# Signs of the second layer's weights put back by VectorE as bits, three small steps free to run on ScalarE or VectorE, and the order drawn anew

## The chip, the cores and the metric

The kernel runs on one core of a Trainium2 chip. A time is the device time of that core in microseconds (us). TensorE (PE) multiplies, VectorE (DVE), ScalarE (ACT) and GpSimd (POOL) do the elementwise work, and SyncE (SP) issues the DMA transfers. TensorE's clock has two levels, 2.4 and 1.2 GHz; the profile gives the granted clock as a share of the upper one.

## The reference, cut to what matters

```python
def reference(q, k, v, w_in, w_out, g_ln, w2_in, w2_out):   # q, k, v: 8 x 8 heads x 576 x 64
    k_p, v_p = mean over groups of 8 positions of k, v       # 72 of them
    attn = softmax(q @ k_p.T / sqrt(64)) @ v_p
    x = attn laid out as 4608 tokens x 512
    h = x @ w_in                                             # 512 x 1024
    solu = h * softmax(h)
    x = (solu - mean) / sqrt(var + 1e-6) * g_ln @ w_out      # 1024 x 512
    h = x @ w2_in                                            # 512 x 2048
    return (h * sigmoid(1.702 * h)) @ w2_out                 # 2048 x 512
```

The inputs arrive as 64-bit floats. A weight is read as pairs of 32-bit words (high word, low word), and a float32 value is made from them in the kernel.

## The kernel before, in words

Each float32 operand of a product is split into two half-precision parts (a high and a low half), and a product is three matmuls (high by high, high by low, low by high).

**The first phase** holds the attention, the first layer and the preparation of the second layer's weights. It runs over 36 tiles of 128 tokens. For a tile t: the scores (TensorE into PSUM tile `psx`), their maximum and the exponential `e`, the sum `rs` of a row of it, `rs` scaled and inverted, `e` times that, its split into the tile `st`, a transposing DMA into `aT`, the product with the values (into PSUM tile `psv`, of which there is one buffer), and its split into the halves of `xT`. Then the first layer's product (into `psh`), its softmax and statistics (`hmx`, `he`, `tt`, `mean`), and for each pair of tiles the normed `zs`, a transposing DMA into `zT`, the product with `w1o` (into `psy`, one buffer) and a copy `y` of it that goes to DRAM.

Weights are prepared beside that. Of a piece `raw` of 128 x 1024 pairs of words ScalarE makes the signs (`sgw`), turns the low words into integers and scales the high words; VectorE shifts and joins them (`scalar_tensor_tensor raw<-raw`), which drops the sign; GpSimd multiplies by `sgw`. For the second layer there are 16 such pieces (`values_of`); the result `w_f` is then combined on GpSimd into seven sums, split into `hi` and `lo`, and written to DRAM as `w2i_dram` and `w2o_dram`. For the first layer (`joined`) there are six more. The scale of a weight needs the largest value of all partitions: a diagonal tile `diag` of the partitions' values is multiplied by ones into `psy` or `psv` (a **spread product**), from where VectorE takes the maximum (`w1o_all`, `galln`, `w2all`, `v_all`).

**The order** of the first phase is drawn by a planner (`Plan`). Every chain of steps is a strand with a due time. `Plan.run` looks at each strand's next operation, estimates from a table of costs when its engine could begin it, adds a part of the slack and a random amount (`DRAWS`: until which planned time of TensorE, how much, which seed), and takes the lowest score. An operation that may run on two engines goes where planned end plus `spare` is earlier. The result is one fixed instruction stream for each engine: an engine runs its stream in order, and an instruction whose input is not there holds up all behind it.

**The second phase** (`Up`, `Down`, from line 1349) is the second layer, written out by hand in blocks of 768 tokens. The change doesn't touch it.

Of the kernel before, what the change touches and what calls it, by code (L numbers as in the profile page):

```python
# [9 lines left out]
F32 = mybir.dt.float32  # L10
F16 = mybir.dt.float16
BF16 = mybir.dt.bfloat16
I32 = mybir.dt.int32
U32 = mybir.dt.uint32
AF = mybir.ActivationFunctionType
ALU = mybir.AluOpType
# [4 lines left out]
P = 128  # L21
# [9 lines left out]
KM = DM // P  # L31
# [11 lines left out]
WC = 512  # L43
# [21 lines left out]
PULL = 900  # L65
HASTE = 0.01
DUE_W_OUT = 40000
SPARE = 3000
DUE_Q = 0
PULL_EARLY = 2  # L70
EARLY_END = 60000
# [5 lines left out]
ALONE = 4  # L77
UPS = 4
DNS = 7
SG = 4  # L80
LAST = 90000
LATE = 3000
LATE_TURN = 3000
TTS = 4
DRAWS = ((70e3, 600, 13), (200e3, 150, 4), (330e3, 150, 13), (1e9, 150, 1))
V_TOP = 2.0 ** 14

TOP3 = 2.0 ** -29 * (1 - 2.0 ** -23)
A_TOP = 2.0 ** 14
# [2 lines left out]
Y_TOP = 2.0 ** 13  # L92
G_DOWN = 2.0 ** -22
TINY = 2.0 ** -100

# [86 lines left out]
class Plan:  # L184
# [31 lines left out]
    def drop(self, *tiles):  # L216
        for t in tiles:
            del self.ring_of[t.name]
# [12 lines left out]
    def estimate(self, op):  # L231
        best = None
        for engine in op.engines:
            t = max(self.free[engine], self.ready(op, engine))
            if engine == "sp":
                t = max(t, self.free["dma"] - 2000)
            if engine == "dve" and op.port and self.pool_from <= t < self.free["pool"]:
                t = self.free["pool"]
            key = t + op.cost[engine] + self.spare[engine] if len(op.engines) > 1 else t
            if best is None or key < best[0]:  # L240
                best = (key, t, engine)
        return best[1:]
# [54 lines left out]
def moe_kernel(ctx: ExitStack, tc: tile.TileContext, qT, kT, vT, w_in, w_out, g_ln, w2_in, w2_out, eye, outT):  # L297
    nc = tc.nc
# [137 lines left out]
    with ExitStack() as ph:  # L436
# [6 lines left out]
        kv = tc.alloc_tile_pool(name="kv", bufs=2, side="right")  # L443
# [12 lines left out]
        plan = Plan()  # L456
        start, drop = plan.start, plan.drop
# [53 lines left out]
        def V(name, *args, **kw):  # L511
            return op(("dve",), name, args, kw)

        def G(name, *args, **kw):
            return op(("pool",), name, args, kw)
# [4 lines left out]
        def A(**kw):  # L520
            return op(("act",), "activation", (), kw)

        def D(dst, src=None, turn=False, short=1):
            pairs = dst if src is None else [(dst, src)]

            def emit(engine):
                for pair in pairs:
                    (nc.sync.dma_start_transpose if turn else nc.sync.dma_start)(*pair)

            outs, ins = ([p[i] for p in pairs] for i in range(2))  # L530
            n = sum(math.prod(x.shape) * mybir.dt.size(x.dtype) for x in outs)
            return Op(("sp",), emit, outs, ins, {"sp": n / 360 * (1.23 if turn else short)}, turn)
# [82 lines left out]
        def values_of(raw, up, dst, begun=None):  # L615

            hw, lw = raw[:, :, 1], raw[:, :, 0]
            sg = yield New(kv, [P, 2 * WC], F16, "sgw", bufs=SG // 2)
            if begun is not None:
                begun.append(sg)  # L620
            yield A(out=sg, in_=hw.bitcast(F32), func=AF.Sign)
            yield A(out=lw.bitcast(U32), in_=lw.bitcast(U32), func=AF.Copy, scale=TOP3, bias=-0.49999)
            yield lambda: (up.name, up.offset) in upped
            yield A(out=hw.bitcast(F32), in_=hw.bitcast(F32), func=AF.Copy, scale=up)
            yield V(
                "scalar_tensor_tensor", out=lw, in0=hw, scalar=3, in1=lw, op0=ALU.logical_shift_left,
                op1=ALU.bitwise_or,
            )
            d = yield from dst()
            yield G("tensor_tensor", out=d, in0=sg, in1=lw.bitcast(F32), op=ALU.mult)  # L630
            drop(sg)

        def raw_new(q, n):
            return New(kv, [P, q, n, 2], I32, "raw", "raw", RAWS)
# [155 lines left out]
        def pooled(kind, b, src, due):  # L790
            yield lambda: b == 0 or begun[kind][b - 1] == 2
            dst = yield New(kv, [P, NPAIR, SP], F32, kind + "p", bufs=1)
# [9 lines left out]
            ps = yield New(psy, [P, 2, YB], F32, "psy", "psy")  # L802
            sums = ps.rearrange("p a c -> p (a c)")[:, : NPAIR * SP].rearrange("p (a s) -> p a s", s=SP)
            for j in range(2):
# [2 lines left out]
                yield T(rows[:4])  # L807
                yield T(rows[4:])
                drop(raws[j])
            yield A(out=dst, in_=sums, func=AF.Copy)  # L810
            drop(ps)
            return dst

# [43 lines left out]
        def attention(t):  # L857
# [10 lines left out]
            ps = yield New(psx, [P, 2, 512], F32, "psx", "psx")  # L868
# [23 lines left out]
            else:  # L892
                yield V(
                    "tensor_tensor", out=e.rearrange("p (a h) k -> p a h k", a=2), in0=s4,
                    in1=m3.unsqueeze(3).to_broadcast([P, 2, 4, SP]), op=ALU.add,
# [2 lines left out]
                yield A(out=e, in_=e, func=AF.Exp)  # L898
            rs = s1("rs", H)
            yield V("tensor_reduce", out=rs, in_=e, axis=AX.X, op=ALU.add)  # L900
            yield A(out=rs, in_=rs, func=AF.Copy, scale=1.0 / A_TOP, bias=1e-9 / A_TOP)
            yield V("reciprocal", rs, rs)
            yield VG("tensor_tensor", out=e, in0=e, in1=rs.unsqueeze(2).to_broadcast([P, H, SP]), op=ALU.mult)
            yield lambda: t < 2 or turned[t - 2]
# [38 lines left out]
            drop(aT)  # L943
            xT = yield New(sb, [P, 2 * KM, P], F16, "xT", bufs=2)
            turned_x = ps.rearrange("p (k t) -> p k t", t=P)
            yield A(out=xT[:, 0:KM], in_=turned_x, func=AF.Copy, scale=1.0 / A_TOP)
            yield V(
                "scalar_tensor_tensor", out=xT[:, KM:], in0=turned_x, scalar=1.0 / A_TOP, in1=xT[:, 0:KM],
                op0=ALU.mult, op1=ALU.subtract,
# [4 lines left out]
        class Pair:  # L954
# [95 lines left out]
            def project(self, half):  # L1050
# [20 lines left out]
                        ]  # L1071
                    )
                y = yield New(sb, [P, 2, YB], F32, "y", bufs=2)
                yield A(out=y, in_=ps, func=AF.Copy)
                drop(drop_ps)
                i, o = divmod(self.i * YB, YD)
                yield D(y_dram[i][:, 2 * half : 2 * half + 2, o : o + YB], y)
# [210 lines left out]
            yield D(eye_t, eye)  # L1288

        plan.early, plan.until = PULL_EARLY, EARLY_END  # L1290
        plan.pull, plan.haste, plan.spare = PULL, HASTE, {"pool": 0.0, "dve": SPARE}

        def due(t):
            return FIRST_STEP + STEP * t
# [430 lines left out]
```

## Time and profile before

| | us |
|---|---|
| median of 3 runs | 1175.5 (1172.25 to 1175.65) |
| the profiled execution | 1171.01 |
| its span in the profile | 1169.0 |
| TensorE busy | 1125.7 (96% of the span) |
| ScalarE, VectorE, GpSimd busy | 754.7, 724.4, 617.7 |

The times in the rows are microseconds from the start of the span. An instruction's idle time stands in brackets with what released it. The second phase begins at about 505 us.

### The profile page before, as it was taken

To read this page: it belongs to the slowest core of one execution; us is meant where nothing else is said; L and a number is where in the kernel's file an instruction comes from. 1 tells how busy PE (TensorE), PEld (TensorE's weight loads), DVE (VectorE), ACT (ScalarE), POOL (GpSimd) and SP (SyncE) were. 2 spreads that over 40 slices of the span, in tenths; PEclk is the share of its full clock that TensorE was granted. 3 is DMA by queue.
4 is the path that set the end of the run, shared out by engine and by line. 5 is a ranking of instruction groups with operands and counts; after the bars stand their busy time and mean duration, and the time that the engine had idled before them with its cause. 6 is when DMAs were issued, how large, how long until landed. Compare 5 with 4: busy or idle time off the path is not lost.

```text
span 1169.0 us, 19696 instructions
## 1 busy us (share of the span) xinstructions
PE 1125.7 (96%) x7737; PEld 726.1 (62%) x7737; DVE 724.4 (62%) x1105; ACT 754.7 (65%) x997; POOL 617.7 (53%) x643
## 2 busy tenths in 40 slices
PE   4888999999999999999999999999999999999998
PEld 4555676667676667765566656666666665566655
DVE  7988888777677753426753773567266636753650
ACT  6889998989798874737624752674367337625740
POOL 4566999989999985315503530561056016403530
PEclk9989999999999999999999999999999999999999
DMA  9979999999999768355465355536453653463131
GB/s 356 277 191 278 243 280 282 278 275 273 270 244 226 178 172 262 85 195 193 146 200 174 125 176 163 180 127 202 142 174 126 214 178 127 149 202 117 60 121 60
DMA packets 247356, 225.75 MB, mean 193 GB/s; under 512 B 165728, under 2 KB 218080, under 8 KB 246752
## 3 DMA queue, kind: packets, MB, share of 16 engines
q1 hardware_dynamic: 247264, 224.50, 67.0%
q8 instruction: 60, 0.98, 0.3%
q14 instruction: 32, 0.26, 0.1%
HBM read 151.06 MB, written 33.55 MB: 158 GB/s over the span
## 4 chain that ended last, share of the span: by engine, by line
PE 69%; POOL 13%; ACT 6%; DVE 5%; DMA 5%; issue 2%; SPq 1%; POOLq 0%; ACTq 0%; DVEq 0%
PE bank_a L1385 31%; PE bank_d L1385 16%; PE bank_b L1385 8%; PE psy L537 6%; PE psh L537 5%; POOL w_f L496 3%; PE psv L537 2%; POOL lo L496 2%; POOL zs L496 2%; POOL st L496 1%; POOL e L496 1%; PE psx L537 1%; DMA w2i_dram<-lo 1%; POOL q L496 1%; DMA raw<-w_out 1%
## 5 line engine op out<-in xcount | busy, mean ns | idle before, releaser
L1385 PEld LDWEIGHTS <-w2o 128*128 128x128 f16 x2016 | 197.0, 98 | 130.4
L1385 PEld LDWEIGHTS <-w2i 128*128 128x128 f16 x1974 | 193.1, 98 | 129.9 <-issue 2.4
L349 POOL TENSOR_TENSOR w_g<-w_g 128x384 f32<-128x384 f32 x42 | 46.1, 1097 | 399.2 <-ACT w_g L1464 399.2
L1479 DVE SCALAR_TENSOR_TENSOR g<-w_g,gu_b,g 128x1152 f16<-128x1152 f32 (+1 forms) x96 | 175.4, 1828 | 92.0 <-ACT g L1474 91.7
L1385 PE MATMUL bank_a<-ys,w2i 128*128 128x384 f16 x1128 | 205.6, 326 | 0.9 <-ACT c L1404 0.9
L537 PE MATMUL psh<-w1i,xT 128*128 128x512 f16 x864 | 201.8, 384 | 3.5 <-ACT xT L496 3.1
L1385 PE MATMUL bank_a<-g,w2o 128*128 128x384 f16 x1152 | 201.6, 326 | 0.0
L537 PEld LDWEIGHTS <-w1o 128*128 128x128 f16 x1728 | 168.0, 98 | 30.8 <-DMA zT<-zs 2.8
L537 PE MATMUL psy<-zT,w1o 128*128 128x256 f16 x1536 | 176.2, 273 | 3.5 <-DMA zT<-zs 2.3
L1474 ACT ACTIVATE g<-w_g,gu_b 128x1152 f16<-128x1152 f32 (+1 forms) x96 | 134.3, 1411 | 50.3 <-POOL w_g L352 39.3
L1404 ACT ACTIVATE c<-bank_a 128x384 f32<-128x384 f32 x188 | 90.7, 483 | 102.4 <-PE bank_a L1385 101.8
L537 PEld LDWEIGHTS <-xT 128*128 128x128 f16 x864 | 83.4, 99 | 96.3 <-issue 6.0
L1385 PE MATMUL bank_d<-g,w2o 128*128 128x384 f16 x576 | 104.2, 326 | 0.0
L496 POOL TENSOR_TENSOR zs<-tt,zs 128x1024 f16<-128x1024 f32 x36 | 78.4, 2178 | 44.2 <-ACT zs L496 43.8
L1385 PE MATMUL bank_d<-ys,w2i 128*128 128x384 f16 x564 | 101.1, 326 | 0.0
L1464 ACT ACTIVATE w_g<-c,ch_b 128x1536 f32<-128x1536 f32 x47 | 73.8, 1570 | 28.7 <-DVE c L1407 28.7
L352 POOL TENSOR_TENSOR w_g<-w_g 128x384 f32<-128x384 f32 x42 | 83.2, 1982 | 0.0
L1407 DVE SCALAR_TENSOR_TENSOR c<-bank_d,c 128x384 f32<-128x384 f32 x94 | 51.9, 552 | 41.9 <-ACT c L1404 29.6
L496 POOL TENSOR_TENSOR lo<-w_f,hi 128x512 f16<-128x512 f32 (+1 forms) x48 | 65.8, 1389 | 6.6 <-ACT e L496 2.9
L496 DVE TENSOR_REDUCE hmx<-psh 128x1 f32<-128x1024 f32 x36 | 43.8, 1218 | 36.2 <-PE psh L537 36.2
L537 PE MATMUL psx<-kbd,qt 128*128 128x144 f32 (+1 forms) x320 | 47.8, 312 | 15.1 <-ACT kbd L496 9.6
L496 DVE CUSTOM_DVE_ANT_0 tt<-psh,he 128x1024 f32<-128x1024 f32 x36 | 43.8, 1218 | 23.1 <-ACT he L496 22.9
(205 smaller groups left out, 1606.8 us busy)
## 6 DMA issues: line engine op xcount, KB each, us to landing
w2i<-w2i_dram SPq DMA_DIRECT2D x48, 896.0 KB, 4.6
w2o<-w2o_dram SPq DMA_DIRECT2D x84, 512.0 KB, 3.7
half<-kT SPq DMA_DIRECT2D x16, 576.0 KB, 6.4
half<-vT SPq DMA_DIRECT2D x16, 576.0 KB, 6.2
qt<-qT SPq DMA_DIRECT2D x36, 256.0 KB, 4.7
y_dram<-y SPq DMA_DIRECT2D x36, 256.0 KB, 3.5
y<-y_dram SPq DMA_DIRECT2D x48, 192.0 KB, 4.0
raw<-w_in SPq DMA_DIRECT2D x16, 512.0 KB, 7.7
```

Source lines behind the costliest of these rows:

```text
L349: eng.tensor_tensor(out=w[:, 1], in0=q[:, Q12], in1=q[:, Q11], op=ALU.subtract)
L352: eng.tensor_tensor(out=w[:, 3], in0=q[:, Q21], in1=w[:, 2], op=ALU.subtract)
L496: getattr(eng, name)(*args, **kw)
L537: nc.tensor.matmul(*p[:3], start=p[3], stop=p[4], skip_group_check=len(p) > 5)
L1385: nc.tensor.matmul(bank, self.weight(p, kk, w), self.data(p, kk, i), start=(first and kk == 0 and w == 0 and i == 0), stop=(last and kk == ...
L1404: nc.scalar.activation(out=self.c[:, i], in_=getattr(self, bank), func=AF.Copy, scale=self.scale)
L1407: nc.vector.scalar_tensor_tensor(out=self.c[:, i], in0=getattr(self, bank), scalar=self.scale, in1=self.c[:, i], op0=ALU.mult, op1=ALU.add,)
L1464: nc.scalar.activation(out=self.w[:, 0:4], in_=self.c, func=AF.Gelu_apprx_sigmoid, scale=self.ch)
L1474: nc.scalar.activation(out=self.g[s.start][:, 0], in_=self.w[:, s], func=AF.Copy, scale=self.gu)
L1479: nc.vector.scalar_tensor_tensor(out=self.g[s.start][:, 1], in0=self.w[:, s], scalar=self.gu, in1=self.g[s.start][:, 0], op0=ALU.mult, op1 ...
```

## The change

The signs of the 16 second-layer pieces are no longer made by ScalarE and multiplied in by GpSimd. After the join, a second `scalar_tensor_tensor` on VectorE takes the sign bit of the high word and ors it into the joined word, on its way from `raw` to `w_f`. The first layer's six pieces keep their `sgw`, now with four buffers in place of two. Three kinds of operations that were ScalarE's alone may now be put on VectorE by the planner, with a reserve (`SPARE_ACT`) of 500: the copies out of PSUM into `y` and the pooled keys and values, the first half of `xT`, and the scaling of `rs`. The seeds of the draws are new, and there are six stretches of them in place of four.

```diff
+SPARE_ACT = 500
-SG = 4
+SG = 8
-DRAWS = ((70e3, 600, 13), (200e3, 150, 4), (330e3, 150, 13), (1e9, 150, 1))
+DRAWS = (
+    (70e3, 600, 15), (160e3, 150, 15), (320e3, 150, 777820), (360e3, 150, 313302), (450e3, 150, 383972),
+    (1e9, 150, 372027),
+)
+SIGN = -(2 ** 31)
...
-            key = t + op.cost[engine] + self.spare[engine] if len(op.engines) > 1 else t
+            key = t + op.cost[engine] + self.spare[op.engines[0], engine] if len(op.engines) > 1 else t
...
+        def AD(out, in_, scale=None):
+            def emit(engine):
+                if engine == "act":
+                    nc.scalar.activation(out=out, in_=in_, func=AF.Copy, **({} if scale is None else {"scale": scale}))
+                elif scale is None:
+                    nc.vector.tensor_copy(out, in_)
+                else:
+                    nc.vector.tensor_scalar_mul(out, in_, scale)
...
+        def rescaled(rs):
+            def emit(engine):
+                if engine == "act":
+                    nc.scalar.activation(out=rs, in_=rs, func=AF.Copy, scale=1.0 / A_TOP, bias=1e-9 / A_TOP)
+                else:
+                    nc.vector.tensor_scalar(
+                        out=rs, in0=rs, scalar1=1.0 / A_TOP, scalar2=1e-9 / A_TOP, op0=ALU.mult, op1=ALU.add
+                    )
...
         def values_of(raw, up, dst, begun=None):
-            sg = yield New(kv, [P, 2 * WC], F16, "sgw", bufs=SG // 2)
-            yield A(out=sg, in_=hw.bitcast(F32), func=AF.Sign)
...
-            yield G("tensor_tensor", out=d, in0=sg, in1=lw.bitcast(F32), op=ALU.mult)
-            drop(sg)
+            yield V(
+                "scalar_tensor_tensor", out=d.bitcast(I32), in0=hw, scalar=SIGN, in1=lw, op0=ALU.bitwise_and,
+                op1=ALU.bitwise_or,
+            )
...
-            yield A(out=dst, in_=sums, func=AF.Copy)
+            yield AD(dst, sums)
...
-            yield A(out=rs, in_=rs, func=AF.Copy, scale=1.0 / A_TOP, bias=1e-9 / A_TOP)
+            yield rescaled(rs)
...
-            yield A(out=xT[:, 0:KM], in_=turned_x, func=AF.Copy, scale=1.0 / A_TOP)
+            yield AD(xT[:, 0:KM], turned_x, 1.0 / A_TOP)
...
-                yield A(out=y, in_=ps, func=AF.Copy)
+                yield AD(y, ps)
```

What the planner made of it, counted over the instruction streams: of 36 scalings of `rs` 17 stand on VectorE, of 36 copies `y` 8, of the 36 first halves of `xT` 1, of the copies of pooled keys and values 2. On GpSimd the 16 products with `sgw` are gone and 2 of 48 `lo` have moved to VectorE; in return GpSimd has 2 more products `e` (36), 1 more `st` (36) and 5 more sums `w_f` (64), which VectorE had.

The streams differ from the first instructions on. Three places follow; the order's rows count a float32 matmul once where the trace has two.

On TensorE, the place where the scales of `w_out` and `g_ln` are spread (`psy<-diag`; the next user of `psy` can begin when the one before has been read). Before, both spread products stand together, behind one `psx`:

```order
L537 MATMUL psx<-kbd_134,qt 128x144 x4
L537 LDWEIGHTS ones
L537 MATMUL psy<-diag_638,ones 128x128
L537 LDWEIGHTS ones
L537 MATMUL psy<-diag_712,ones 128x128
L537 LDWEIGHTS xT
```

In the changed kernel:

```order
L567 MATMUL psh<-w1i_127,xT 128x512
L567 LDWEIGHTS ones
L567 MATMUL psy<-diag_737,ones 128x128
L567 MATMUL psx<-kbd_134,qt 128x144 x4
L567 MATMUL psy<-half,eye_t 128x144 x8
...
L567 MATMUL psy<-half,eye_t 128x144 x8
L567 LDWEIGHTS ones
L567 MATMUL psy<-diag_751,ones 128x128
L567 LDWEIGHTS vst_131
```

The two spread products now stand apart, with two groups of pooled keys (`psy<-half`) and four `psh` and two `psx` groups between them; the second stands directly behind such a group.

On SyncE, the DMA queue, at the first pair's transposes `zT` (`raw<-w_in` here are loads of the second layer's weights, two for each half of a piece). Before:

```order
L528 DMA_TRANSPOSE aT<-st_136 128x16x128
L528 DMA qt<-qT 128x512
L528 DMA raw<-w_in 128x4x256 x6
L528 DMA qt<-qT 128x512
L528 DMA raw<-w_in 128x4x256 x2
L528 DMA_TRANSPOSE zT<-zs 128x16x128 x2
```

In the changed kernel:

```order
L558 DMA_TRANSPOSE aT<-st_136 128x16x128
L558 DMA qt<-qT 128x512
L558 DMA_TRANSPOSE zT<-zs 128x16x128 x2
L558 DMA_TRANSPOSE aT<-st_135 128x16x128
L558 DMA_TRANSPOSE aT<-st_136 128x16x128
L558 DMA raw<-w_in 128x4x256 x2
```

The eight loads of `raw` have moved from ahead of the `zT` transposes to behind them.

On VectorE, in front of a low half of `xT`, in the part where the second layer's weights are prepared. Before (the place of rows 11 below):

```order
L496 SCALAR_TENSOR_TENSOR raw<-raw 128x1024 x2
L496 TENSOR_REDUCE mx<-psx 128x8
L496 TENSOR_TENSOR e<-psx,mx 128x576
L496 SCALAR_TENSOR_TENSOR xT<-psv,xT 128x512
L496 TENSOR_REDUCE hmx<-psh 128x1
```

In the changed kernel, at such a place:

```order
L501 TENSOR_REDUCE w2a_150<-w2am 128x1
L501 SCALAR_TENSOR_TENSOR raw<-raw 128x1024
L501 SCALAR_TENSOR_TENSOR w_f<-raw 128x1024
L501 SCALAR_TENSOR_TENSOR raw<-raw 128x1024
L501 SCALAR_TENSOR_TENSOR xT<-psv,xT 128x512
L501 TENSOR_REDUCE mx<-psx 128x8
L501 TENSOR_REDUCE hmx<-psh 128x1
```

Three operations of 128 x 1024 words stand in a row ahead of the half of `xT`, where two stood; one of them is the new one.

## Rows read from the trace of the kernel before

**Rows 1.** The page, part 1: engine, busy us, share of the span, instructions.

```profile
PE 1125.7 (96%) x7737; PEld 726.1 (62%) x7737; DVE 724.4 (62%) x1105; ACT 754.7 (65%) x997; POOL 617.7 (53%) x643
```

**Rows 2.** Windows: stretch, its us, busy us by engine (instructions), clock, DMA, GB/s.

```profile
0.00:36.00 36.00, 14.80 (x82) 13.25 (x82) 26.23 (x47) 25.10 (x35) 18.57 (x25) 1.00 0.99 338
...
60.00:120.00 60.00, 51.80 (x378) 33.58 (x376) 53.61 (x116) 54.87 (x84) 38.89 (x56) 0.94 0.94 237
120.00:480.00 360.00, 351.79 (x2837) 244.75 (x2836) 250.12 (x453) 296.52 (x432) 316.96 (x373) 1.00 0.97 242
...
505.00:1169.00 664.00, 659.07 (x4066) 397.18 (x4063) 362.32 (x436) 343.54 (x404) 224.42 (x168) 1.00 0.46 155
```

**Rows 3.** Waits of PE, 60 to 505 us: us in total, times, longest.

```profile
PE psv L537 <- DVE xT L496: 4.6, 6, 1.7
...
PE psv L537 <- DVE w2all L496: 2.2, 1, 2.2
```

**Rows 4.** Timeline of PE, 0 to 60 us: start, us, instructions, idle before and releaser.

```profile
36.06 2.59 PE L537 MATMUL psh<-w1i,xT 128*128 128x512 f16 x6 [3.12 <-ACT xT L496]
```

**Rows 5.** Timeline of PE, 60 to 130 us.

```profile
69.07 0.22 PE L537 MATMUL psy<-diag,ones 128*128 128x128 bf16 x1 [2.41 <-ACT kp L496]
71.40 0.27 PE L537 MATMUL psy<-diag,ones 128*128 128x128 bf16 x1 [2.11 <-DVE mean L496]
...
102.08 5.41 PE L537 MATMUL psy<-zT,w1o 128*128 128x256 f16 x48 [2.34 <-DMA zT<-zs]
```

**Rows 6.** Windows of 5 us after two idle stretches of PE.

```profile
70.00:75.00 5.00, 3.60 (x12) 2.13 (x12) 3.86 (x21) 4.31 (x7) 4.15 (x9) 0.54 0.68 165
75.00:80.00 5.00, 5.00 (x25) 3.21 (x25) 3.81 (x7) 2.88 (x5) 1.65 (x5) 0.78 0.76 154
300.00:305.00 5.00, 2.90 (x41) 2.74 (x41) 3.49 (x11) 3.12 (x6) 4.92 (x8) 0.75 1.15 272
305.00:310.00 5.00, 5.00 (x36) 2.28 (x35) 4.25 (x8) 3.62 (x6) 4.84 (x10) 0.91 1.09 359
```

**Rows 7.** Timeline of all engines, 62 to 72 us.

```profile
64.66 2.02 DVE L496 SCALAR_TENSOR_TENSOR raw<-raw 128x1024 int32<-128x1024 int32 x1
...
65.55 2.28 POOL L496 TENSOR_TENSOR st<-e,st 128x576 f16<-128x576 f32 x1
...
68.63 0.39 ACT L496 ACTIVATE kp<-psy 128x288 f32<-128x288 f32 x1
```

**Rows 8.** Timeline of the DMA queue, 84 to 103 us: issues.

```profile
90.23 9.57 SPq L528 DMA_TRANSPOSE zT<-zs  x2
```

**Rows 9.** Timeline of all engines, 297 to 303 us.

```profile
299.31 1.22 DVE L496 TENSOR_REDUCE w2am<-raw 128x1 f32<-128x1024 f32 x1 [2.63 <-DMA raw<-w_out]
...
302.10 0.83 PE L537 MATMUL psv<-aT,vst 128*64 128x64 f16 x32 [2.20 <-DVE w2all L496]
```

**Rows 10.** Groups over the span: busy us, mean ns, idle before.

```profile
L496 POOL TENSOR_TENSOR w_f<-sgw,raw 128x1024 f32<-128x1024 f16 x16 | 34.6, 2161 | 0.2
...
L496 ACT ACTIVATE sgw<-raw 128x1024 f16<-128x1024 f32 x22 | 25.1, 1143 | 6.3 <-POOL w_f L496 4.9 <-POOL raw L496 1.3
L496 DVE SCALAR_TENSOR_TENSOR xT<-psv,xT 128x512 f16<-128x512 f32 x36 | 24.7, 687 | 12.4 <-ACT xT L496 12.1
...
L496 ACT ACTIVATE y<-psy 128x512 f32<-128x512 f32 x32 | 18.8, 587 | 16.5 <-PE psy L537 14.4 <-PE psx L537 2.1
...
L496 ACT ACTIVATE rs<-rs 128x8 f32<-128x8 f32 x36 | 7.2, 201 | 1.1 <-DVE rs L496 0.9
L496 DVE RECIPROCAL rs<-rs 128x8 f32<-128x8 f32 x36 | 7.1, 197 | 5.0 <-ACT rs L496 4.8
```

**Rows 11.** Timeline of all engines, 218 to 228 us.

```profile
222.54 2.02 DVE L496 SCALAR_TENSOR_TENSOR raw<-raw 128x1024 int32<-128x1024 int32 x1 [3.08 <-ACT raw L496]
...
226.75 0.64 PE L537 MATMUL psv<-aT,vst 128*64 128x128 f16 x16 [1.68 <-DVE xT L496]
```

**Rows 12.** Tile raw on VectorE, 60 to 480 us: ns min/median/max, first, last.

```profile
L496 DVE SCALAR_TENSOR_TENSOR raw<-raw x18: 1209/1546/2218, 62.1 to 399.8; 128x1024 int32<-128x1024 int32 x18
```

More of the change, by code (lines that the diff above doesn't have):

```diff
@@ L521, in A @@
             return op(("act",), "activation", (), kw)
+        def AD(out, in_, scale=None):
[6 more added lines that the diff above has]
+                    nc.vector.tensor_scalar_mul(out, in_, scale)
+            costs = {"act": cost("act", "activation", [out], [in_]), "dve": cost("dve", "tensor_copy", [out], [in_])}
+            return Op(("act", "dve"), emit, [out], [in_], costs)
+        def rescaled(rs):
[6 more added lines that the diff above has]
+                    )
+            return Op(("act", "dve"), emit, [rs], [rs], {"act": 200, "dve": 150})
         def D(dst, src=None, turn=False, short=1):
@@ L617, in values_of @@
             hw, lw = raw[:, :, 1], raw[:, :, 0]
-            sg = yield New(kv, [P, 2 * WC], F16, "sgw", bufs=SG // 2)
             if begun is not None:
-                begun.append(sg)
-            yield A(out=sg, in_=hw.bitcast(F32), func=AF.Sign)
+                begun.append(raw)
             yield A(out=lw.bitcast(U32), in_=lw.bitcast(U32), func=AF.Copy, scale=TOP3, bias=-0.49999)
@@ L1290, in moe_kernel @@
         plan.early, plan.until = PULL_EARLY, EARLY_END
-        plan.pull, plan.haste, plan.spare = PULL, HASTE, {"pool": 0.0, "dve": SPARE}
+        plan.pull, plan.haste, plan.spare = PULL, HASTE, {("pool", "pool"): 0.0, ("pool", "dve"): SPARE, ("act", "act"): 0.0, ("act", "dve"): SPARE_ACT}
         def due(t):
```

## The prediction

> **What bounds the kernel now.** The page first: TensorE is busy for 96% of the span, the three elementwise engines for 53 to 65% [rows 1]. The windows show where its idle time lies [rows 2]: 21.2 us up to 36 us, before the first layer's products can begin; 8.2 us from 60 to 120 us; 8.2 us from 120 to 480 us; and under 5 us in the second phase, 664 us long, which the change leaves as it is. So the change can win or lose only in the first 505 us, and the most that it can win there is the idle time after the start, 16.4 us, and what low clocks cost.
>
> The shares of the other engines in the stretch from 120 to 480 us are the reason why order matters at all there: GpSimd 317 of 360 us, ScalarE 297, VectorE 250 [rows 2]. TensorE's waits are short and spread: of the nine rows of the waits from 60 to 505 us none names GpSimd; the largest sum is 4.6 us for the halves of `xT`, in 6 pieces [rows 3]. Two places cost more than the rest. From 66 to 71 us TensorE stands still twice in front of the two spread products, 2.41 us for ScalarE's copy `kp` and 2.11 us for VectorE [rows 5], and then runs at a granted clock of 0.54 and 0.78 for two windows of 5 us, after which it is at full speed [rows 6]. At 302 us it waits 2.20 us for `w2all`, because VectorE sits in front of `w2am` until a load of `raw` has landed [rows 9]; the clock is 0.75 and 0.91 behind it [rows 6]. Such a window is a mixture of 1.2 and 2.4 GHz. Taken as work not done they cost at most 0.46 x 5 + 0.22 x 5 = 3.4 us and 0.25 x 5 + 0.09 x 5 = 1.7 us. One more wait of size is 2.34 us for the first `zT` [rows 5], whose transposes were issued at 90.23 us and held the queue for 9.57 us [rows 8], behind eight loads of `raw`.
>
> **What the change moves, by engine.** Signs: GpSimd loses 16 products of 2.161 us, 34.6 us; ScalarE loses 16 of its 22 signs at 1.143 us, 18.3 us [rows 10]. VectorE gets 16 operations that the trace does not show in this form. The nearest is the join itself, two inputs of the same size: 1.21 us at least, 1.55 us in the middle, 2.22 us at most [rows 12]. I take the middle, 24.8 us; the bounds are 19.4 and 35.5 us. Copies: 8 of the `y` leave ScalarE (0.587 us each, 4.7 us) for VectorE, where a one-input read of PSUM of that size is not shown; the half of `xT` reads the same amount in 0.687 us [rows 10], and between half of that and all of it the 8 cost 2.7 to 5.5 us; I take 5.5. Of the scalings of `rs` 17 leave ScalarE (0.201 us, 3.4 us); on VectorE they cost about a reciprocal of that shape, 0.197 us [rows 10], 3.3 us, and spare a hand-over to ScalarE and back. The two `lo` that VectorE gets, the few sums and products that it gives back, and the one half of `xT` and two small copies are under 4 us each way. In the stretch from 120 to 480 us this makes VectorE some 280 us busy, GpSimd some 286 and ScalarE some 273 of 360. No one of these sums is on TensorE's path; by themselves I cost them at nothing, because all three engines still have over 70 us free there, while TensorE has 8. What they change is how late an instruction stands in its stream, and that is paid at single places.
>
> **The sum, place by place**, against the profiled execution, 1171.0 us. The median of the runs shown is 1175.5 us, 4.5 above it, so I take the difference over to that.
>
> 1. The two spread products. Now 4.5 us of waiting and up to 3.4 us of clock. VectorE and ScalarE were late here: a join took 2.02 us beside a GpSimd `st` of 2.28 us, and `kp` came at 68.63 us, behind an exponential [rows 7]. In the new order the products stand apart, with two groups of pooled keys, four of `psh` and two of `psx` between them, so that the second no longer waits for the maximum of the first; but the second stands directly behind a group whose copy has to be made first. That costs at least one copy and its hand-overs, about 1 us, and at most what `kp` cost now, 2.4. I take 1.5 us and no fall of the clock: a gain of 6.4 us. Bounds: nothing (the wait and the clock's fall move with it) to 7.9.
> 2. The first `zT`. Its transposes move ahead of the eight loads. Gain 2.3 us; bounds 0 and 2.3.
> 3. The wait at 302 us. A buffer of `raw` is now free when VectorE has read it, not when GpSimd, which has hardly any idle time ahead of these products (0.2 us in all [rows 10]), has come to them. So loads can be issued earlier, but `w2am` still stands in VectorE's stream. I take half of 2.2 + 1.7: 2.0 us; bounds 0 and 3.9.
> 4. VectorE's longer stream. At 222.54 us one join took 2.02 us ahead of a half of `xT`, and TensorE waited 1.68 us for it [rows 11]. That is one of 18 joins [rows 12], and 16 more like them come, at the place shown above as the third in a row. At the same rate: 16 / 18 x 1.68 = 1.5 us lost. Bounds: 0, and 27 us if each of the 16 did so.
> 5. The start. The first half of the keys is now loaded behind one of the values, which delays the first scores, and a row sum and a half of `xT` stand in front of the reciprocal that the scale of `w_in` needs, 0.69 us of VectorE for the half [rows 10] and, as an estimate, as much for the sum. Against that, products with the pooled values now stand ahead of the first `psh`, where TensorE waits 3.12 us today [rows 4]. I take a loss of 1.5 us; bounds: a gain of 3 and a loss of 3.
>
> Sum: -6.4 - 2.3 - 2.0 + 1.5 + 1.5 = -7.7 us. 1171.0 becomes 1163.3, and the median 1175.5 becomes 1167.8, say 1168. With the bounds of terms 1 to 3 and 5 alone the result lies between -17 and +3 before term 4.
>
> **The rivals.**
>
> A. The forecast, 4 to 12 us faster: 1163.5 to 1171.5. Chance 0.55.
>
> B. The waits are only dealt anew: what terms 1 to 3 give comes back at other places, since the new order has as many close neighbours on `psv` and `psy` as the old one. Within 3.5 us, 1172 to 1179. For it speaks that TensorE's waits are mostly a chain of two engines between two users of one PSUM buffer, which no engine's load explains; against it that the two dear places hold 11.8 of the 21.5 us (waits and clock) that are lost from 60 to 480 us. Chance 0.22.
>
> C. VectorE becomes late, and it is slower. It is the engine that ended most of the waits from 60 to 505 us [rows 3], and it gets the work. The mechanism is the one of term 4: a join stretched beside a GpSimd operation to 2.0 or 2.2 us, with a half of `xT`, a maximum or a spread product's maximum queued behind it. Each such place costs 1.68 us; the 9.2 us that the other four terms give are used up when between five and six of the 16 new operations do it, eight make it 4 us slower, 1180, and all sixteen 18 us, 1193. Against it: the products that GpSimd loses are among those that stretch VectorE, and from 120 to 480 us VectorE stays no fuller than GpSimd. Chance 0.12.
>
> D. It goes better: GpSimd's and ScalarE's relief removes most of the small waits too, and no clock falls are left after 60 us: 13 to 17 us, 1158 to 1162. Chance 0.11.
>
> That the change does not do what it says is no case of its own: the 16 products are gone from the stream. What is small is the freedom on the three other kinds: 8 of 36, 1 of 36, 17 of 36.
>
> A word on C from the pages. The Trainium skill, in "SBUF — State Buffer", section "SBUF: two separate sides", says that VectorE and GpSimd share a pair of ports under an exclusive lock, that a VectorE operation with two SBUF inputs needs it against a GpSimd operation that reads SBUF, and that the loser waits for the whole instruction. The new operation has two SBUF inputs. By that page alone each of the 16 could wait out a `st` of 2.28 us, 36 us more for VectorE, which would be C in full. The trace agrees in kind, with joins from 1.21 to 2.22 us [rows 12], but shows no more than 1.0 us of waiting in one, so the sum goes by the rows.
>
> **How the numbers follow.** The time is that of A. Against no change a measurement of this kernel tells about 0.3%, 3.5 us. Faster by more: A without its edge, and D: 0.65. Within: most of B and A's edge: 0.22. Slower by more: C and a little of B: 0.13. The range has to leave out no more than 2 in 10: it leaves out most of C (above 1178) and the better end of D (below 1159).
>
> **What would show it.** In the trace after: the 16 `w_f<-raw` on VectorE at 1.2 to 2.2 us each and GpSimd's busy time down by about 30 us; no two waits over 2 us around the spread products `w1o_all` and `galln`, and a granted clock of 1.00 in the 10 us behind them; no wait for `zT` of 2 us near 100 us; TensorE's idle time from 60 to 480 us at 8 to 11 us in place of 16.4; the second phase beginning at about 497 us and as long as before. The prediction is wrong if the waits for `xT`, `w2all` and `mean` together grow past 12 us, if the first `psh` begins after 39 us, or if the clock falls at a new place.

## The result: about half a per cent slower

The changed kernel takes 1179.49 us (median of 8 runs, 1176.07 to 1180.61), the kernel before 1172.95 us beside it (8 runs, 1170.98 to 1175.65). The ratio is 1.0051, with a 95% interval from 1.0036 to 1.0066: some 6 us slower, where 7.7 us faster was forecast. The 1175.5 us from which the prediction started are the median of three of these 8 runs of before.

The profiled execution took 1180.61 us, its span is 1178.6 us, 9.6 more than before. It is the slowest of its 8 runs, and the profiled one of before is nearly the fastest, so the two traces lie some 3 us further apart than the medians. The page's part 1 answers to [rows 1]: VectorE's sum rose by 24.7 us, ScalarE's fell by 21.1 and GpSimd's by 19.2, where the prediction had named about 30 for GpSimd. TensorE is as busy as it was.

```profile
PE 1126.6 (96%) x7737; PEld 725.1 (62%) x7737; DVE 749.1 (64%) x1141; ACT 733.6 (62%) x960; POOL 598.5 (51%) x634
```

The windows of after, columns as in [rows 2]:

```profile
0.00:36.00 36.00, 13.73 (x79) 12.44 (x80) 25.87 (x38) 23.11 (x34) 17.21 (x19) 1.00 0.97 352
36.00:60.00 24.00, 23.10 (x166) 16.24 (x165) 22.95 (x47) 21.35 (x29) 16.12 (x19) 0.94 0.97 266
60.00:120.00 60.00, 52.99 (x392) 34.36 (x391) 55.56 (x117) 50.81 (x75) 37.81 (x48) 0.94 0.89 212
120.00:480.00 360.00, 343.79 (x2753) 236.52 (x2752) 270.33 (x487) 273.41 (x395) 291.87 (x369) 0.99 0.99 243
```

From 120 to 480 us TensorE now stands idle for 16.21 us, where it was 8.21 [rows 2]. Up to 36 us it is 22.27 (21.20 before), from 60 to 120 us 7.01 (8.20). So nearly all of the added idle time lies in the long stretch, although VectorE, ScalarE and GpSimd are busy there for 270, 273 and 292 of 360 us, close to the 280, 273 and 286 of the prediction, and none of them is as full as GpSimd was. The second phase begins 10.0 us later (its first product into `bank_a` at 524.20 us, before at 514.20) and is as long as it was. The waits of TensorE from 60 to 500 us, columns as in [rows 3], name the causes:

```profile
PE psv L567 <- DVE xT L501: 8.1, 5, 3.9
PE psy L567 <- ACT y L532: 5.0, 4, 2.0
PE psv L567 <- DMA vst<-vx: 3.6, 1, 3.6
PE psv L567 <- DVE w2all L501: 2.6, 3, 1.4
```

The waits for `xT` were 4.6 us [rows 3] and are 8.1. Those for `y`, which were 1.1 us in sum, and the one for `vst`, which did not exist, come to 8.6.

**The places of the prediction.** The timeline of TensorE in after, columns as in [rows 4]; the rows stand at the second spread product, behind it, at the first `zT` and at the new wait for `vst`:

```profile
81.70 0.23 PE L567 MATMUL psy<-diag,ones 128*128 128x128 bf16 x1 [1.21 <-DVE vp L534]
...
87.64 1.06 PE L567 MATMUL psv<-aT,vst 128*64 128x128 f16 x16 [3.91 <-DVE xT L501]
...
103.18 1.05 PE L567 MATMUL psy<-zT,w1o 128*128 128x256 f16 x8
...
187.92 0.63 PE L567 MATMUL psv<-aT,vst 128*64 128x64 f16 x28 [3.64 <-DMA vst<-vx]
```

The second spread product does wait little, 1.21 us. But 6 us behind it TensorE waits 3.91 us for `xT`, and then its clock falls. The windows behind the waits at 87.64 and 187.92 us and behind one of 2.03 us at 242.79 us:

```profile
85.00:90.00 5.00, 2.36 (x20) 1.37 (x21) 4.96 (x8) 4.75 (x8) 4.95 (x4) 0.69 0.57 130
90.00:95.00 5.00, 5.00 (x17) 1.89 (x16) 5.00 (x9) 4.90 (x8) 2.60 (x4) 0.63 1.22 271
...
190.00:195.00 5.00, 5.00 (x31) 3.43 (x30) 4.79 (x9) 2.91 (x6) 3.73 (x5) 0.73 1.09 329
...
245.00:250.00 5.00, 5.00 (x38) 4.05 (x37) 4.97 (x11) 4.28 (x7) 1.62 (x4) 0.77 0.95 217
```

A fall of the clock at a new place was one of the signs that the prediction had named against itself; and TensorE's idle time from 60 to 480 us is 23.2 us, not 8 to 11.

What VectorE does ahead of 87.64 us is a queue, in the timeline of all engines:

```profile
83.36 0.74 DVE L501 TENSOR_REDUCE rs<-e 128x8 f32<-128x576 f32 x1
84.13 0.54 DVE L547 TENSOR_SCALAR rs<-rs 128x8 f32<-128x8 f32 x1
...
84.91 1.34 DVE L501 TENSOR_REDUCE kp<-half 128x144 f32<-128x1152 f32 x1
...
86.18 0.68 DVE L536 TENSOR_SCALAR xT<-psv 128x512 f16<-128x512 f32 x1
...
86.89 0.69 DVE L501 SCALAR_TENSOR_TENSOR xT<-psv,xT 128x512 f16<-128x512 f32 x1
```

`psv` was full at 82.55 us (a product of 0.69 us from 81.86). Both halves of `xT` are made by VectorE here; the first is the one that the change took from ScalarE. Both stand behind a row sum, a scaling and the sum `kp`, 1.34 us, which nobody waits for at once.

### The profile page after: what moved, and what is told of

It reads as the page before. It is cut to its first block, busy times and chain, and to the rows that moved or that the text cites. A ratio compares the mean times of both kernels' runs of the same rounds, so it can differ in the third digit from the quotient of the medians.

```text
span 1178.6 us, 19704 instructions
## 1 busy us (share of the span) xinstructions
PE 1126.6 (96%) x7737; PEld 725.1 (62%) x7737; DVE 749.1 (64%) x1141; ACT 733.6 (62%) x960; POOL 598.5 (51%) x634
## 4 chain that ended last, share of the span: by engine, by line
PE 69%; POOL 9%; DVE 8%; ACT 6%; DMA 4%; issue 3%; SPq 0%; POOLq 0%; ACTq 0%; DVEq 0%
PE bank_a L1415 31%; PE bank_d L1415 15%; PE bank_b L1415 8%; PE psh L567 6%; PE psy L567 6%; PE psv L567 2%; POOL lo L501 2%; POOL st L501 1%; POOL w_f L501 1%; POOL e L501 1%; DMA half<-kT 1%; POOL zs L501 1%; PE psx L567 1%; DVE rs L501 1%; DMA vst<-vx 1%
## 5 line engine op out<-in xcount | busy, mean ns | idle before, releaser
L567 PE MATMUL psy<-zT,w1o 128*128 128x256 f16 x1584 | 183.7, 275 | 5.0 <-ACT y L532 5.0
L567 PEld LDWEIGHTS psx<-kbd,qt 128*128 128x128 f32 (+1 forms) x320 | 41.3, 192 | 25.5 <-ACT kbd L501 11.2
```

The costliest lines, as they stand in the source:

```text
L567: nc.tensor.matmul(*p[:3], start=p[3], stop=p[4], skip_group_check=len(p) > 5)
```

## The experiments

Two theories stood after this comparison, and a third joined them on the way; the expectations number them. Theory 1: VectorE's new work costs the time, that is the small scalings of `rs`, far dearer than priced, and the 16 second joins. Theory 2: the order as drawn has its waits at other places, whatever VectorE does. Theory 3, from the fifth kernel on: the order of either kernel is a picked one, and another draw costs more than the exchange of operations. To part operations from order, several kernels keep an order instruction by instruction, with only the operation exchanged at its place: the planner still plans the old operation, and only its `emit`, which issues the instruction, is replaced. The others keep the operations and draw the order with other seeds. Each ratio is to the kernel before on the same chip, and a difference of two kernels is taken from their ratios, times 1173 us.

**The scalings on ScalarE, in the order of after.**

```diff
         def rescaled(rs):
             def emit(engine):
-                if engine == "act":
+                if True:
```

> The changed kernel with its order kept as planned on every engine; only the 17 scalings of rs that stand on VectorE are done by ScalarE at the same place of the order. Theory 1 (VectorE's new work, stretched beside GpSimd, is what made the changed kernel 6 us slower than before): the 17 scalings took 11.4 us on VectorE in the trace after, where I had counted 3.3, so taking them away gives back 2 to 4 us, and the kernel comes out 2 to 4 us slower than before. Theory 2 (the order as drawn has its waits at other places, whatever VectorE does): within 1.5 us of the changed kernel, so 4.5 to 7.5 us slower than before.

Measured: 1183.07 us, 1.0093 [1.0078, 1.0108], some 5 us slower than after. The waits of TensorE from 60 to 500 us show where:

```profile
PE psy L567 <- ACT y L532: 8.5, 4, 3.5
PE psv L567 <- DVE xT L501: 8.4, 5, 4.5
```

The scalings are stretched on VectorE, but in this order ScalarE has no room for them: the waits for `y`, which is ScalarE's, are longer by 3.5 us in sum. Neither theory had expected this. The run does not say what the stretched scalings cost where they are, only that ScalarE is no better place for them in this order.

**No second join, in the order of after.** The one join that is left stands at the second one's place, and the signs of the second layer's weights are left out.

```diff
-            yield V(
+            join = V(
                 "scalar_tensor_tensor", out=lw, in0=hw, scalar=3, in1=lw, op0=ALU.logical_shift_left,
                 op1=ALU.bitwise_or,
             )
+            join.emit = lambda engine: None
+            yield join
...
+            second.emit = lambda engine: nc.vector.scalar_tensor_tensor(
+                out=d.bitcast(I32), in0=hw, scalar=3, in1=lw, op0=ALU.logical_shift_left, op1=ALU.bitwise_or
+            )
```

> The changed kernel with its order kept as planned; of the two joins of each of the 16 second-layer pieces only one is issued, at the place of the second and straight into w_f, so that the sign is left out of these weights. VectorE has 16 operations fewer, about 23 us. Theory 1: this gives back 3 to 6 us, and the longest waits for halves of xT after 120 us (2.03 us at 243 us) go; 0 to 3 us slower than before. Theory 2: within 1.5 us of the changed kernel.

Measured: 1173.79 us, 1.0013 [1.0002, 1.0024]. By the ratios the 16 joins cost 0.0038 x 1173 = 4.5 us in this order. The waits and the two places:

```profile
PE psv L567 <- DVE xT L501: 5.8, 3, 3.9
PE psv L567 <- DVE w2all L501: 4.1, 3, 3.4
...
PE psy L567 <- ACT y L532: 1.4, 1, 1.4
```

```profile
87.52 1.06 PE L567 MATMUL psv<-aT,vst 128*64 128x128 f16 x16 [3.90 <-DVE xT L501]
...
186.40 0.96 PE L567 MATMUL psv<-aT,vst 128*64 128x64 f16 x28 [3.51 <-DMA vst<-vx]
```

The waits for `xT` and `y` shrink by 5.9 us, and the one of 2.03 us is gone, as theory 1 had it; a part comes back elsewhere, above all in a wait of 3.4 us for `w2all`. The two longest of after, here 3.90 and 3.51 us, stay as they were: they belong to the order and not to the joins, as theory 2 had it.

**All that the planner may move, on ScalarE**: the scalings, the copies `y` and of pooled values, the first half of `xT`; order of after. The edit stands twice, in `AD` and in `rescaled`.

```diff
-                if engine == "act":
+                if True:
```

> The changed kernel with its order kept as planned; the 17 scalings of rs, the 8 copies y, the 2 copies of pooled keys and values and the one first half of xT that stand on VectorE are all done by ScalarE at the same place of the order. What is left of the change is the signs by VectorE and the new draws. Theory 1: 3 to 5 us given back, 1 to 3 us slower than before; but ScalarE gets some 9 us of work at places that were not planned for it. Theory 2: within 2 us of the changed kernel, either way.

Measured: 1180.08 us, 1.0065 [1.0048, 1.0082], not to be told from after. VectorE is relieved by 7 us in the long stretch (263.13 us busy against 270.33 there) and it buys nothing: in its place stand `xT` with 10.8 us of waits and `y` with 6.1. The wait behind the second spread product does not go, although the first half of `xT` is ScalarE's again; it grows:

```profile
89.02 1.06 PE L567 MATMUL psv<-aT,vst 128*64 128x128 f16 x16 [5.27 <-DVE xT L501]
```

**The changed kernel with the old seeds, and the old kernel with the new seeds.**

```diff
-DRAWS = ((70e3, 600, 15), (160e3, 150, 15), (320e3, 150, 777820), ...
+DRAWS = ((70e3, 600, 13), (200e3, 150, 4), (330e3, 150, 13), (1e9, 150, 1))
```

> The changed kernel with the seeds and stretches of the draws of before; the order is drawn anew with the changed operations. Theory 1: the work is the same, so it stays 3 to 8 us slower than before. Theory 2: another order, and so another time, that may lie anywhere from 4 us faster to 8 us slower than before; a time within 2 us of before, or faster, speaks for it. It also shows how far one draw lies from another: under 2 us from the changed kernel would mean that draws matter little.

> The kernel before with the seeds and stretches of the changed kernel and nothing else of the change. The changed operations with the old draws came out 21 us slower than before, so a draw now seems to be worth more than any operation. Theory 3 (each of the two kernels has a picked order; with any other draws either design is 10 to 25 us slower): 10 to 25 us slower than before. Theory 1 (the work given to VectorE is what costs): the old operations need not suffer from new draws, within 4 us of before.

Measured: 1193.40 us, 1.0181 [1.0166, 1.0196], and 1184.54 us, 1.0092 [1.0065, 1.0118]. The first lies beyond what theories 1 and 2 had allowed, the second at the lower end of what theory 3 had. Seeds that serve one set of operations do not serve the other. The old operations in another order are slower than after.

**The bits in the order of before**: no sign on ScalarE, and at the place of each product VectorE's second join; no other instruction moves.

```diff
-            yield A(out=sg, in_=hw.bitcast(F32), func=AF.Sign)
+            sign = A(out=sg, in_=hw.bitcast(F32), func=AF.Sign)
+            sign.emit = lambda engine: None
+            yield sign
...
-            yield G("tensor_tensor", out=d, in0=sg, in1=lw.bitcast(F32), op=ALU.mult)
+            bits = G("tensor_tensor", out=d, in0=sg, in1=lw.bitcast(F32), op=ALU.mult)
+            bits.emit = lambda engine: nc.vector.scalar_tensor_tensor(
+                out=d.bitcast(I32), in0=hw, scalar=-(2 ** 31), in1=lw, op0=ALU.bitwise_and, op1=ALU.bitwise_or
+            )
+            yield bits
```

> The kernel before with its order kept as planned on every engine; the 16 signs of the second layer's pieces are not made by ScalarE, and the 16 products of GpSimd are replaced, at the same place of the order, by VectorE's second join. Theory 1: VectorE gets 23 us more in an order that had not counted on it, and this is slower than before by 3 to 8 us. Theory 3: the exchange by itself is worth little against a draw, and the relief of GpSimd (34.6 us) and ScalarE (18.3 us) counts as much as VectorE's load; 3 us faster to 2 us slower than before.

Measured: 1177.17 us, 1.0019 [1.0005, 1.0032], 2.2 us slower than before, between the ranges of theory 3 (up to 2) and theory 1 (from 3).

**The product in the order of after**: the sign is made in front of the low words' conversion on ScalarE, and GpSimd multiplies at the place of the second join.

```diff
+                nc.scalar.activation(out=sg[0], in_=hw.bitcast(F32), func=AF.Sign)
...
+            second.emit = lambda engine: nc.gpsimd.tensor_tensor(out=d, in0=sg[0], in1=lw.bitcast(F32), op=ALU.mult)
```

> The changed kernel with its order kept as planned; the signs of the 16 pieces are made by ScalarE ahead of the low words, and GpSimd multiplies by them at the place of VectorE's second join. Theory 1: VectorE is relieved of 23 us, as in the run without the second joins, which gave back 5.7 us; 2 to 6 us faster than the changed kernel, about as before. Theory 3: GpSimd and ScalarE get 35 and 18 us that this order had not counted on; 2 to 15 us slower than the changed kernel.

Measured: 1187.67 us, 1.0115 [1.0089, 1.0141], 7.5 us slower than after, as theory 3 had it; theory 1 had expected 2 to 6 us faster.

**Four seeds that nobody chose (101 to 104), for either kernel; and seeds picked for each of them, among some hundreds, by the end of its plan.**

```diff
+DRAWS = ((70e3, 600, 101), (200e3, 150, 102), (330e3, 150, 103), (1e9, 150, 104))
```

> The kernel before with its own stretches and amounts of draws and four other seeds, chosen without looking. Theory 3: 8 to 25 us slower than before. Theory 1 says nothing of it; draws that matter little would leave it within 4 us of before.

> The changed kernel with the four other seeds and the stretches that the kernel before had in its run with other draws (8 to 16 us slower than before). Theory 3 (the draw decides, and the two designs are equal over draws): 8 to 20 us slower than before, within 8 us of that run. Theory 1 (VectorE's new work costs by itself): 15 to 25 us slower, clearly behind that run.

> The kernel before with draws that its planner, by its own table of costs, likes best among some 700 sets, with the stretches of the changed kernel. Theory 3: a draw picked so is as good as the changed kernel's, 3 to 10 us slower than before, and the order of before is a rare one; theory 1: as good as before or better, since the old operations with a good order are what the plan thinks they are, 6 us faster to 2 us slower.

> The changed kernel with draws picked in the same way among some 500 sets. Theory 3: within 4 us of the run of before with picked draws, 2 to 10 us slower than before. Theory 1: 5 us or more behind that run.

Measured, old operations: 1188.86 us (two runs, 1.0127 [1.0068, 1.0185]) and 1185.23 us (1.0104 [1.0069, 1.0139]). Changed operations: 1198.62 us (two runs, 1.0209 [1.0168, 1.0249]) and 1182.43 us (1.0072 [1.0048, 1.0095]). With the seeds of before and of after that makes four pairs: the changed operations come out worse under the first seeds of before and under 101 to 104, better under the new seeds and among the picked ones. Two of these runs went against theory 3: the old operations with picked seeds are 12.2 us slower, beyond its 10, and the changed ones under 101 to 104 are 24.5 us slower, 9.6 behind the old ones, which is what theory 1 had expected (with two runs each, the 9.6 us are uncertain by some 8). Four pairs that do not agree do not say that one set of operations is better over the orders. Over the orders the old operations range over 14.9 us and the changed ones over 18.5, more than the exchange moves in a fixed order (2.2 and 7.5 us).

**The scaling planned as one that shares GpSimd's port**, seeds picked anew.

```diff
-            return Op(("act", "dve"), emit, [rs], [rs], {"act": 200, "dve": 150})
+            return Op(("act", "dve"), emit, [rs], [rs], {"act": 200, "dve": 150}, port=True)
```

> The changed kernel with one correction to its plan: the scaling of rs on VectorE is planned as an operation that waits until GpSimd's instruction has ended, as the trace after shows it (0.16 to 1.77 us), and with draws picked in the same way. If the plan's blindness to that wait is a part of the loss, this is 2 to 6 us faster than the changed kernel with picked draws, and may come within 2 us of before; if not, within 2 us of it.

Measured: 1178.66 us, 1.0046 [1.0032, 1.0061]. Only 7 scalings are left on VectorE, and most of them are short; in their tile's rows stand ns min/median/max, first and last start:

```profile
L551 DVE TENSOR_SCALAR rs<-rs x7: 157/171/810, 68.9 to 406.2; 128x8 f32<-128x8 f32 x7
```

That is the time of after, within the intervals. Against the changed kernel with picked seeds it is 3.0 us faster, inside the 2 to 6 us by which the expectation would know that the plan's blindness to this wait has a part in the loss. But the two intervals overlap, and the order is another one, so that stays open.

**The relief alone, in the order of before**: ScalarE's signs and GpSimd's products are left out, and with them the second layer's signs; the one join stands at the product's place.

```diff
+            sign.emit = lambda engine: None
...
+            join.emit = lambda engine: None
...
+            product.emit = lambda engine: nc.vector.scalar_tensor_tensor(
+                out=d.bitcast(I32), in0=hw, scalar=3, in1=lw, op0=ALU.logical_shift_left, op1=ALU.bitwise_or
+            )
```

> The kernel before with its own order kept, and the 16 products on GpSimd and the 16 signs on ScalarE left out: the one join that stands at each product's place writes w_f itself, so the second layer's signs are not put back (that is the part of the computation left out). It takes 34.6 us of GpSimd and 18.3 us of ScalarE out of the stretch up to 505 us, and adds nothing. Theory 3 (the engines beside TensorE have slack in this order, and the order alone decides): within 2 us of before, 1171 to 1175. Theory that the relief is worth something by itself: 3 us or more faster than before, 1170 or less. Against the run of the order of before with 16 signs put back by VectorE (1.0019) the difference is the price of the 16 second joins in this order: by theory 3 about 2 us, against 5.7 us in the order of after.

Measured: 1169.25 us, 0.9967 [0.9953, 0.9981], 3.9 us faster. This is beyond the 2 us of the third theory: relief is worth something by itself. Against the bits in the same order, the 16 second joins cost 0.0052 x 1173 = 6.1 us, where theory 3 had about 2. The waits of TensorE from 60 to 500 us, first with no signs at all, then with the bits:

```profile
PE psv L537 <- DVE w2all L496: 3.5, 3, 2.7
...
PE psv L537 <- DVE xT L496: 2.3, 3, 1.3
...
PE psy L537 <- ACT y L496: 1.6, 2, 0.9
```

```profile
PE psv L537 <- DVE xT L496: 7.6, 7, 3.3
PE psy L537 <- ACT y L496: 5.0, 5, 2.0
```

With the product they are 4.6 and 1.1 us [rows 3]. The same two groups grow with the joins here as they do in the order of after.

## Why the prediction was wrong

The kernels in a fixed order make a table; each entry is the difference to before in us, the ratio less one times 1173:

| | no sign | product | bits |
|---|---|---|---|
| order of before | -3.9 | 0 | +2.2 |
| order of after | +1.5 | +13.5 | +6.0 |

The order of after includes the copies and scalings that it deals out; with all of them on ScalarE the entry of the bits is +7.6 in place of +6.0, so they are not what makes that order dear. Read along the rows it gives the price of an operation, down the columns the price of the order. The intervals of the entries are 1.3 to 3 us to either side.

**The step that failed** is the one that turned terms 1, 2, 3 and 5 into the forecast A: that repairing the places of before which could be seen to be dear gives -9.2 us. With the bits in either, the new order costs +3.8 us against the old one, with no sign +5.4, with the product +13.5. Each place was reckoned in the old order, and only what the new order does there was asked, not what it does elsewhere; the largest new waits, 3.91 us for `xT` and 3.64 us for `vst`, have nothing of their size in the waits of before, where `xT` reaches 1.7 us [rows 3] and no wait for `vst` stands from 60 us on. Rival B said this, that the waits are dealt anew, and had 0.22. It was priced as an even exchange; three other orders of the old operations cost 10.8 to 14.9 us. So the order of before was not one among equals: as far as these three tell, a new one was to be expected worse, and neither the shares of busy time nor any row of before says so. That is the largest error.

**Term 1** (spread products, -6.4) came out at its bound of nothing, and in the way that the bound described. The waits at the two products went from 4.5 us to 0.42 and 1.21, but 3.91 us stand right behind. The windows at 85 and 90 us have clocks of 0.69 and 0.63, which taken as before are 0.31 x 5 + 0.37 x 5 = 3.4 us, what it was at 70 us [rows 6]. Wait and fall moved on by 17 us. The wait is there with one join, too (3.90 us), and with all the moved operations back on ScalarE (5.27 us), so it is the queue in the order.

**Term 2** (`zT`, -2.3) held: the row at 103.18 us has no wait. But another transfer costs more than that: `vst` was issued at 177.70 us, as soon as VectorE had written its input (177.67 us), landed 10.2 us later, where the eight of before took 3.1 to 7.1 us, and TensorE waited 3.64 us for it. What made it so late is not shown.

**Term 3** (`w2all`, -2.0): no single wait over 1.4 us is left, and the sum is 2.6 us against 2.2. The fall of the clock at 300 us is gone, but one of 0.73 and one of 0.77 stand in other places.

**Term 4** (VectorE's longer stream, +1.5) was too small: 4.5 us in one order and 6.1 in the other. Rival C's mechanism is there. The timeline of all engines in after:

```profile
237.79 2.13 POOL L501 TENSOR_TENSOR zs<-tt,zs 128x1024 f16<-128x1024 f32 x1 [1.04 <-ACT zs L501]
237.87 3.14 DVE L501 SCALAR_TENSOR_TENSOR w_f<-raw 128x1024 int32<-128x1024 int32 x1
...
239.89 2.13 POOL L501 TENSOR_TENSOR lo<-w_f,hi 128x512 f16<-128x512 f32 x1
...
240.93 1.21 DVE L501 TENSOR_REDUCE hmx<-psh 128x1 f32<-128x1024 f32 x1
...
242.06 0.67 DVE L501 SCALAR_TENSOR_TENSOR xT<-psv,xT 128x512 f16<-128x512 f32 x1
...
242.79 0.23 PE L567 MATMUL psv<-diag,ones 128*128 128x128 bf16 x1 [2.03 <-DVE xT L501]
```

The join takes 3.14 us, the half of `xT` stands behind it and a maximum, and TensorE waits 2.03 us; with one join this wait is gone. But it is the only one over 2 us behind a second join in after; the rest of the price is in smaller waits, for `xT` and, as the kernels without second joins show in both orders, for ScalarE's `y`. That the joins delay `y` through what VectorE hands to ScalarE is argued, not shown. The rate of one dear place in 18 joins had left the small ones out.

One reading behind term 4 and rival C was wrong as well. The join of 2.02 us in [rows 7] was stretched not by `st` but by a product of the first layer ahead of it. That product ended at 65.61 us, the join 1.07 us later at 66.68, and `st` 1.15 us after the join, at 67.83. The product in the timeline of before, and the group of all `st` of GpSimd there (busy us, mean ns, idle before):

```profile
63.44 2.17 POOL L496 TENSOR_TENSOR raw<-sgw,raw 128x1024 f32<-128x1024 f16 x1 [1.90 <-DVE raw L496]
```

```profile
L496 POOL TENSOR_TENSOR st<-e,st 128x576 f16<-128x576 f32 x35 | 46.5, 1329 | 7.7 <-ACT st L496 7.4
```

So the 2.28 us of that `st` hold its own wait for the join. With the mean of 1.33 us the 36 us of the prediction's estimate would have been some 21.

**What I costed at nothing** was the second error: "no one of these sums is on TensorE's path". GpSimd's 34.6 us and ScalarE's 18.3 us give 3.9 us when taken away in the order of before, and 12.0 us in that of after. Term 4 and this partly cancel, +2.2 us in the order of before, which is near the 1.5 us of the sum, for the wrong reason. In the order of after the exchange is a gain of 7.5 us; that this order was drawn with the bits in it is the likely reason, but not a shown one.

**Term 5** (the start, +1.5) held: by the windows up to 60 us TensorE is idle for 23.17 us, 1.9 more than before, and the first `psh` begins at 41.84 us, past the 39 us that the prediction named as a sign against itself.

**The small edits.** The copies `y` cost 5.5 us on VectorE, as priced, the joins 23.5 us (24.8 priced). The scalings of `rs`, priced at 3.3 us, cost 11.4:

```profile
L501 DVE SCALAR_TENSOR_TENSOR w_f<-raw 128x1024 int32<-128x1024 int32 x16 | 23.5, 1471 | 0.4 <-POOL lo L501 0.2
...
L547 DVE TENSOR_SCALAR rs<-rs 128x8 f32<-128x8 f32 x17 | 11.4, 671 | 0.3
...
L534 DVE COPY y<-psy 128x512 f32<-128x512 f32 x8 | 5.5, 683 | 0.9 <-PE psy L567 0.9
```

The reciprocal of that shape was the wrong nearest row. The trace of before had a better one, a scaling of four columns, seen among VectorE's groups over the span:

```profile
L409 DVE TENSOR_SCALAR ch_b<-ch,y_dn 128x4 f32<-128x4 f32 x6 | 1.3, 220 | 0.0
...
L496 DVE TENSOR_SCALAR ch<-w2i_dn,co 128x4 f32<-128x4 f32 x1 | 1.2, 1215 | 0.0
```

The same kind of operation and the same shape, 0.22 us in one place and 1.22 in another. It is not shown to have decided the result: in this order ScalarE is no better place, as the first experiment shows.

What stays open is why the order of before is so good. The runs show that it is better than the four others tried with the old operations (after's seeds, 101 to 104, the picked ones, and that of after itself with the product), not which of its neighbourhoods does it. No kernel here that computes the whole beats it.

## What to carry to other kernels

Where one stream per engine is drawn anew, do not add up the places that the new order repairs: compare orders with the operations held fixed, and expect that a new order brings waits at places which the trace of before cannot show. Price an exchange of operations on both sides in one fixed order, work taken away as well as work added: a neighbour engine with 12 to 31% of free time still delays TensorE through the hand-overs. And before a small step is moved to VectorE, look for the longest instruction of its kind in the trace, not for the mean of one with its shape.

## What the runs showed of the hardware

VectorE and GpSimd shut each other out for whole instructions here. The join at 237.87 us ended at 241.01, which is 1.09 us after GpSimd's `zs` ended at 239.92, and alone it takes 1.17 us (the least of the 16). GpSimd's next `lo`, from 239.89 us, ended 1.01 us after the join, and one of that shape takes 1.16 us at 179.37 us. So first VectorE waited and then GpSimd. In the trace of before the prediction found no more than 1.0 us of waiting; here it is 1.97. The Trainium skill, "SBUF — State Buffer", section "SBUF: two separate sides", says that the one that starts first has the pair of ports for the whole instruction; the trace agrees.

A scaling of only 8 columns does it, too. The 17 scalings take 159 ns at least, 691 in the middle, 1765 at most:

```profile
L547 DVE TENSOR_SCALAR rs<-rs x17: 159/691/1765, 20.4 to 422.4; 128x8 f32<-128x8 f32 x17
```

The one at 84.13 us ended at 84.67, with GpSimd's `zs` (from 82.51 for 2.14 us, to 84.65). All twelve that took over 0.3 us ended so, 0.01 to 0.03 us after a GpSimd instruction; the other five took 0.16 to 0.17 us. The reciprocals of the same shape stay between 183 and 212 ns, all 36, also in the middle of a GpSimd instruction:

```profile
353.50 1.65 POOL L501 TENSOR_TENSOR lo<-w_f,hi 128x768 f16<-128x768 f32 x1
...
354.51 0.20 DVE L501 RECIPROCAL rs<-rs 128x8 f32<-128x8 f32 x1
```

The Trainium skill, "VectorE: DVE Perf Modes", section "Mode 2×_2P — use both read ports for one tensor", says that an operation with one input, from SBUF to SBUF, can use both read ports even for float32, and names scaling and copying as such. By that and by the section on SBUF of the Trainium skill named above, the scaling is one that waits for the lock, and the trace agrees; that the reciprocal is not, only the trace shows.
